# Attention with forget gates, then a GELU layer: another decay, another order of the first two batches

## The chip, the cores and the metric

The kernel runs on one core of a Trainium2 chip. The metric is the device time in microseconds, the median of several runs. In the text PE is TensorE (PEld its weight loads), DVE is VectorE, ACT is ScalarE, POOL is GpSimd, and SP is the engine that issues most of the plain DMAs.

## What is computed

Eight batches of causal attention with a decay, eight heads of 64 numbers, 576 positions; then two dense layers with an exact GELU between them on all 4608 rows. The reference, cut:

```python
scores = q @ k.T / sqrt(D)                       # q, k, v: (8, 8, 576, 64); f: (8, 8, 576)
cum    = cumsum(log(clip(f, 1e-4, 1.0)), -1)
decay  = cum[..., :, None] - cum[..., None, :]
attn   = softmax(where(causal, -1e9, scores + decay))
x      = (attn @ v) as rows of 512               # 8 heads side by side
h      = x @ w_in                                # (512, 2048)
out    = (0.5 * h * (1 + erf(h / sqrt(2)))) @ w_out   # (2048, 512)
```

In a softmax row the part of the decay that depends on the query cancels. So both kernels only weigh the key side: each row of v, and the column of ones beside it that yields the sum of the row, is multiplied by a weight of its key, and the division at the end takes out any common factor.

## The kernel before, as far as it is touched

Names. A pair `i` is two heads; `scores(b, i, t)` makes score tile `t` (of four) of pair `i`, keys on the partitions, in one of two score buffers in PSUM, and its exponential on ACT. Causal masks are either added by PE inside the tile (two small products with `key_of` and `after` for each 128-wide diagonal block) or cut out by POOL after the exponential (`affine_select`). `attend` is AV, 15 products of 65 columns for a head; `normalize` divides on DVE; `to_xT` transposes x for the dense layer. gemm1 is the first dense layer, gemm2 the second.

The decay:

```python
nc.vector.tensor_scalar(f_sb, f_sb, 1e-4, 1.0, Alu.max, Alu.min)
nc.scalar.activation(lf, f_sb, Act.Ln)
nc.vector.tensor_tensor_scan(cum, ones, lf, 0.0, Alu.mult, Alu.add)
# ... cut: in first_attention(), after the transposes of pair 0
nc.scalar.activation(wk, cum, Act.Exp, bias=cum[:, S // 2 : S // 2 + 1], scale=-1.0)
```

The second half of batch 0's attention:

```python
transposes_first(0, 3, 0, m_psum, "m")
scores(0, 2, 0)
transposes_first(0, 3, 1, m_psum, "m")     # PE transposes, then a DVE copy into kT[3]
weigh_v(0, 0, nc.vector)                   # one tensor_tensor of 640 columns
weigh_v(0, 1, nc.vector)
gate(0, 4)                                 # POOL reads v, so what follows waits for it
load_w_in(0); load_w_in(1)
weigh_v(0, 2); weigh_v(0, 3)               # POOL
load_w_in(2)
# ... cut
load_v(1, 0, 4)
load_w_in(3)
load_qk_tokens(1, 0, 4); load_qk_tokens(1, 4, 8)
load_w_out(0)
scores(0, 2, 1)
heads = [(i, h) for i in range(3) for h in range(2)]
for i, t in ((2, 2), (2, 3), (3, 0), (3, 1), (3, 2), (3, 3)):
    scores(0, i, t)
    attend_head(*heads.pop(0))
```

While gemm1 of batch 0 runs (its last quarter), POOL and SP do this:

```python
behind(qk_of[1][0], H - 1)                 # POOL reads the last head of q: waits for its landing
nc.gpsimd.memset(v_sb[:, 4:8, 0, 0:1], 0.0)
load_v(1, 4, 8)                            # SP, behind that memset
weigh_v(1, 0)
load_w_out(1)
weigh_v(1, 1)
load_qk_tokens(2)
```

Batch 1's attention, cut:

```python
tiles(0, 0)                                # score tiles 0 and 1 of pair 0
transposes(1, o_psum, "o"); transposes(2, m_psum, "m"); transposes(3, o_psum, "o")
tiles(0, 2)
take(fill, 2)                              # two products of gemm2_first(0)
tiles(1, 0); run(0); tiles(1, 2)           # run(i): AV of both heads of pair i
take(fill, 4)
weigh_v(1, 2)
tiles(2, 0); run(1)
weigh_v(1, 3)
tiles(2, 2)
take(fill, 4)
tiles(3, 0)
# ... cut: x of pairs 0 and 1 transposed, two more of gemm2
tiles(3, 2)
# ... cut
run(2)
take(fill, 4)
av(3, 0)
to_xT(b, 2, nc.scalar.copy, ps=both[:, 0, 0:XC])   # both: a score buffer
av(3, 1)
gemm1_begin(1, both)
```

`gemm2_first(0)` takes 16 products of 512 columns for batch 0 here: the first eight of sixteen blocks of w_out for two of four row tiles. The rest is done in batch 2's attention by `gemm2_second` (the other eight blocks for those two tiles, in halves of 64 rows) and `gemm2_rows(0, PLAN_0)` (all sixteen for the other two).

Of the kernel before, what the change touches and what calls it, by code (L numbers as in the profile page):

```python
# [15 lines left out]
P = 128  # L16
S = 576
# [36 lines left out]
def kernel(  # L54
# [100 lines left out]
    e4 = [consts.tile([P, 2, 448], BF16, name=f"e4{i}") for i in range(4)]  # L155
    for t in e4:
        nc.gpsimd.memset(t[:, :, 0:D], 0.0)
    diagonal(ident_fp, Alu.not_equal, 1.0, 0)
    load_qk_tokens(0, 6, 8)
# [20 lines left out]
    ones = consts.tile([BH, S], FP32)  # L180
    lf = f_sb
    cum = consts.tile([BH, S], FP32)
    wk = f_sb
    nc.vector.memset(ones, 1.0)
    nc.vector.memset(wT[0:D, 4, :], 0.0)
    nc.vector.tensor_scalar(f_sb, f_sb, 1e-4, 1.0, Alu.max, Alu.min)
    nc.scalar.activation(lf, f_sb, Act.Ln)
    nc.vector.memset(v_sb[0:D, :, 4, :], 0.0)
    nc.vector.tensor_tensor_scan(cum, ones, lf, 0.0, Alu.mult, Alu.add)
    spark = consts.tile([1, 1], FP32)  # L190
    nc.scalar.activation(spark, ones[0:1, 0:1], Act.Exp)

    def warm_up(n):

        ps = m_psum.tile([P, TC], FP32, tag="m", name="ps_w")
        for _ in range(n):
            nc.tensor.matmul(ps, warm[:, 0:P], warm, start=True, stop=True)
# [4 lines left out]
    def transposes_first(b, i, which, pool, tag):  # L202

        src = qk_of[b][which]
        ps = pool.tile([P, JT, PT], BF16, tag=tag, name="ps_f")
        for j in range(JT):
            for h in range(2):
                nc.tensor.transpose(
                    ps[h * D : (h + 1) * D, j, :],
                    src[:, 2 * i + h, j * D : (j + 1) * D],  # L210
                    ident_bf[:PT, :PT],
                )

        dst = (qT, kT)[which][i].rearrange("d (p j) -> d p j", j=JT)
        src = ps.rearrange("d j p -> d p j")
        if b or i:
            nc.vector.tensor_copy(dst, src)
        elif which:
            nc.vector.tensor_copy(dst[:, 0 : PT // 2], src[:, 0 : PT // 2])
            nc.scalar.copy(dst[:, PT // 2 :], src[:, PT // 2 :])  # L220
        else:
            nc.scalar.copy(dst, src)
# [41 lines left out]
    def weigh_v(b, i, eng=nc.gpsimd):  # L264

        hs = slice(2 * i, 2 * i + 2)
        bh = b * H + 2 * i
        w = wT[:, :, bh : bh + 2].rearrange("p n h -> p h n")
        eng.tensor_tensor(  # L269
            vw(b)[:, hs, :, 0:D],  # L270
            v_sb[:, hs, :, :],
            w.unsqueeze(3).to_broadcast([P, 2, NBLK, D]),
            Alu.mult,
        )
        if b:
            eng.tensor_copy(vw(b)[:, hs, :, D], w)
# [3 lines left out]
    def scores(b, i, t):  # L280
        on_pe = b == 0 or (b == 1 and i == 0)
# [42 lines left out]
    def attend(b, i, h, ms):  # L324
        if (b, i, h) not in o_of:
            o_of[b, i, h] = o_psum.tile([P, NBLK, D + 1], FP32, tag="o", name="o")
        o = o_of[b, i, h]
        for m in ms:
            for n in range(m + 1):
                t, c = where(n, m)  # L330
                nc.tensor.matmul(  # L331
                    o[:, m, :],
                    e_of[b, i, t][:, h, c : c + P],
                    vw_of[b][:, 2 * i + h, n, :],
                    start=(n == 0),
                    stop=(n == m),
                )
# [114 lines left out]
    PLAN_0 = [(2, "o", 16 * "r"), (3, "m", 14 * "r" + 2 * "n")]  # L452
# [57 lines left out]
    def gemm2_first(c):  # L510

        pss = [
            m_psum.tile([P, d_model], FP32, tag="m", name="ps2") for _ in range(2)
        ]
        for kq in (0, 4):
            for ts in range(2):
                for kt in range(kq, kq + 4):
                    nc.tensor.matmul(  # L518
                        pss[ts],
                        g_of[c][kt][:, ts * P : (ts + 1) * P],  # L520
                        w_out_sb[:, kt, :],
                        start=(kt == 0),
                        stop=(kt == 7),
                    )
                    if kt == 7:
                        ot_of.append(
                            o_pool.tile([P, d_model], FP32, tag="ot", name="ot")
                        )
                        copy = nc.scalar.copy if ts else nc.vector.tensor_copy
                        copy(ot_of[ts], pss[ts])  # L530
                    yield

    def gemm2_second(c):

        for ts, pool, tag in ((0, o_psum, "o"), (1, m_psum, "m")):
# [3 lines left out]
            for kt in range(8, n_ff):  # L539
                for r in range(2):  # L540
                    rows = slice(r * D, (r + 1) * D)
                    nc.tensor.matmul(  # L542
                        banks[r],
                        g_of[c][kt][rows, ts * P : (ts + 1) * P],
                        w_out_sb[rows, kt, :],
                        start=(kt == 8),
                        stop=(kt == n_ff - 1),
                    )
                if kt == n_ff - 1:
                    nc.vector.tensor_tensor(ot_of[ts], ot_of[ts], banks[1], Alu.add)  # L550
                    sum_out(c, ts, ot_of[ts], banks[0])
                yield

    def gemm2_third():
        yield from gemm2_second(0)
        yield from gemm2_rows(0, PLAN_0)
# [18 lines left out]
    def first_attention():  # L575
# [6 lines left out]
        def attend_head(i, h):  # L582
            attend(0, i, h, (0, 1, 2, 3, 4))
# [4 lines left out]
        nc.scalar.activation(  # L588
            wk, cum, Act.Exp, bias=cum[:, S // 2 : S // 2 + 1], scale=-1.0
        )  # L590
        warm_up(2)
        scores(0, 0, 0)
        scores(0, 0, 1)
        transposes(1, m_psum, "m")
        scores(0, 0, 2)
        psw = o_psum.tile([P, NBLK, BH], FP32, tag="o", name="psw")
        for n in range(NBLK):
            nc.tensor.transpose(
                psw[:, n, :], wk[:, K0[n] : K0[n] + P], ident_fp[:BH, :BH]
# [8 lines left out]
        transposes(2, m_psum, "m")  # L608
        scores(0, 1, 1)
        scores(0, 1, 2)  # L610
# [3 lines left out]
        transposes_first(0, 3, 1, m_psum, "m")  # L614
        weigh_v(0, 0, nc.vector)
# [8 lines left out]
        load_v(1, 0, 4)  # L624
# [5 lines left out]
        heads = [(i, h) for i in range(3) for h in range(2)]  # L630
        for i, t in ((2, 2), (2, 3), (3, 0), (3, 1), (3, 2), (3, 3)):
            scores(0, i, t)
            attend_head(*heads.pop(0))
# [87 lines left out]
    def second_attention():  # L721
# [23 lines left out]
        transposes(1, o_psum, "o")  # L745
        transposes(2, m_psum, "m")
        transposes(3, o_psum, "o")
        tiles(0, 2)
# [4 lines left out]
        take(fill, 4)  # L753
        weigh_v(1, 2)
# [11 lines left out]
        tiles(3, 2)  # L766
        behind(qk_of[2][1], H - 1)
# [4 lines left out]
        av(3, 0)  # L772
        both = s_psum.tile([P, 2, 1024], BF16, tag="s", name="ps_x2")
        to_xT(b, 2, nc.scalar.copy, ps=both[:, 0, 0:XC])
        av(3, 1)
# [4 lines left out]
    for b in range(B):  # L780
# [8 lines left out]
        for ffb in range(4 if b < 2 else 5, n_ff):  # L789
            gemm1(b, ffb, ps=spare() if b > 1 and ffb in (7, 8) else None)  # L790
            if b == 0:
# [3 lines left out]
                if ffb == 12:  # L795
                    behind(qk_of[1][0], H - 1)
                    nc.gpsimd.memset(v_sb[:, 4:8, 0, 0:1], 0.0)
                    load_v(1, 4, 8)
                    weigh_v(1, 0)
                    load_w_out(1)  # L800
                    weigh_v(1, 1)
                    load_qk_tokens(2)
# [43 lines left out]
```

## Time and profile before

| what | value |
|---|---|
| time, median of 3 | 337.49 us (337.18 to 338.54) |
| span of the profiled execution | 335.5 us |
| busy time of DVE, ACT, POOL in the span | 181.2, 209.2, 122.4 us |
| bytes moved by DMA | 44.16 MB, 132 GB/s on average |
| gemm1 of batch 0 starts | 22.97 us |
| gemm1 of batch 1 starts | 55.69 us |

How to read it. The page gives each engine's busy time and, in 40 equal slices of the span, its busy share in tenths. A matmul's record is longer than the time until the next one may start[...]; so a busy PE is not PE at its peak, and the distance between starts tells more. A table by stretch gives busy time between two moments, counted from the start of the span. The timeline lists instructions in order; in brackets stands how long the engine was idle before it, and which engine, line and tile ended that wait. Where several things were waited for, only the last is named. For a DMA the trace has the time of issue and the time of landing.

### The profile page before, as it was taken

To read this page: it belongs to the slowest core of one execution; us is meant where nothing else is said; L and a number is where in the kernel's file an instruction comes from. 1 tells how busy PE (TensorE), PEld (TensorE's weight loads), DVE (VectorE), ACT (ScalarE), POOL (GpSimd) and SP (SyncE) were. 2 spreads that over 40 slices of the span, in tenths; PEclk is the share of its full clock that TensorE was granted. 3 is DMA by queue.
4 is the path that set the end of the run, shared out by engine and by line. 5 is a ranking of instruction groups with operands and counts; after the bars stand their busy time and mean duration, and the time that the engine had idled before them with its cause. 6 is when DMAs were issued, how large, how long until landed. Compare 5 with 4: busy or idle time off the path is not lost.

```text
span 335.5 us, 7820 instructions
## 1 busy us (share of the span) xinstructions
PE 326.8 (97%) x3161; PEld 171.2 (51%) x3161; DVE 181.2 (54%) x414; ACT 209.2 (62%) x299; POOL 122.4 (36%) x250
## 2 busy tenths in 40 slices
PE   8799989999999999999999999999999999999995
PEld 3574546445554456445644565446544654444443
DVE  4770456684358945894589547964696550020011
ACT  6977797773734787378827891788378846404600
POOL 8190286038437044723463343624351420000000
PEclk9999999999999999999999999999999999999998
DMA  7999999989999799599949698689800241011013
GB/s 113 188 166 191 206 172 165 193 157 169 206 197 177 119 198 189 102 141 148 224 120 141 136 179 174 87 158 211 140 35 2 83 64 61 0 66 62 0 41 84
DMA packets 104627, 44.16 MB, mean 132 GB/s; under 512 B 83408, under 2 KB 100048, under 8 KB 104592
## 3 DMA queue, kind: packets, MB, share of 16 engines
q1 hardware_dynamic: 87296, 29.52, 46.4%
q0 software_dynamic: 16896, 13.63, 27.6%
q8 instruction: 24, 0.39, 0.5%
q10 hardware_dynamic: 400, 0.52, 0.4%
q14 instruction: 11, 0.09, 0.1%
HBM read 36.85 MB, written 9.44 MB: 138 GB/s over the span
## 4 chain that ended last, share of the span: by engine, by line
PE 83%; DMA 10%; POOL 3%; issue 1%; ACT 1%; DVE 1%; SPq 0%; POOLq 0%; DVEq 0%; ACTq 0%
PE ps L386 33%; PE ps L482 26%; PE ps L422 8%; PE o L331 7%; PE s L300 6%; DMA w_out_sb<-in_moe_w_out_dram 6%; DMA xT<-x 2%; DMA v_sb<-in_v_dram 2%; PE ps L542 1%; PE ps L518 1%; POOL q L108 1%; POOL k L108 1%; ACT e L310 1%; POOL vw L269 0%; SPq L120 0%
## 5 line engine op out<-in xcount | busy, mean ns | idle before, releaser
L406 ACT ACTIVATE g<-ps 128x512 bf16<-128x512 f32 x144 | 82.1, 601 | 83.7 <-PE ps L386 83.7
L310 ACT ACTIVATE e<-s 128x896 bf16<-128x896 f32 (+2 forms) x128 | 100.1, 835 | 20.9 <-PE s L300 18.2
L386 PE MATMUL ps<-xT,w_in_sb 128*128 128x512 bf16 x512 | 112.7, 379 | 0.1
L482 PE MATMUL ps<-w_out_sb,g 64*128 64x512 bf16 (+1 forms) x711 | 108.1, 377 | 0.0
L386 PEld LDWEIGHTS <-w_in_sb 128*128 128x128 bf16 x576 | 55.9, 98 | 67.8 <-issue 2.1
L312 POOL TENSOR_SCALAR_AFFINE_SELECT e<-e 128x256 bf16<-128x256 bf16 (+1 forms) x135 | 49.3, 386 | 86.9 <-ACT e L310 86.6
L482 PEld LDWEIGHTS <-g 64*128 64x128 bf16 (+1 forms) x711 | 39.4, 95 | 34.7 <-issue 4.2
L269 POOL TENSOR_TENSOR vw<-v_sb,wT 128x640 bf16<-128x640 f32 x30 | 38.7, 1290 | 26.0 <-DMA v_sb<-in_v_dram 14.7
L300 PE MATMUL s<-qT,kT 64*128 64x320 bf16 (+4 forms) x384 | 43.8, 276 | 2.2 <-ACT e L310 1.3
L250 DVE COPY kT<-tk 64x288 bf16<-64x288 bf16 x96 | 43.9, 458 | 2.3 <-DMA tk<-k 0.7
L250 DVE COPY qT<-tq 64x288 bf16<-64x288 bf16 x96 | 38.8, 404 | 3.7 <-DMA tq<-q 2.3
L490 DVE COPY ot<-ps 128x512 f32<-128x512 f32 x20 | 13.8, 692 | 47.2 <-PE ps L482 47.2
L331 PEld LDWEIGHTS <-e 128*128 128x128 bf16 x960 | 34.5, 98 | 8.6 <-POOL e L312 2.5
L331 PE MATMUL o<-vw,e 128*128 128x65 bf16 x960 | 37.4, 194 | 0.5 <-DVE vw L269 0.5
L345 DVE TENSOR_TENSOR x<-o,r 128x320 bf16<-128x320 f32 x64 | 31.5, 492 | 3.3 <-DMA xT<-x 1.1
L431 DVE COPY ot<-ps 128x512 f32<-128x512 f32 (+2 forms) x9 | 5.7, 633 | 49.6 <-PE ps L422 49.6
L300 PEld LDWEIGHTS <-kT 64*128 64x128 bf16 x384 | 19.6, 94 | 24.1 <-issue 7.6
L422 PE MATMUL ps<-w_out_sb,g 128*128 128x512 bf16 (+2 forms) x144 | 28.0, 355 | 0.0
L422 PEld LDWEIGHTS <-g 128*128 128x128 bf16 x144 | 13.5, 98 | 14.5
L344 DVE RECIPROCAL r<-o 128x5 f32<-128x5 f32 x64 | 12.1, 189 | 12.2 <-PE o L331 12.1
L502 DVE TENSOR_TENSOR ot<-ot,ps 128x512 f32<-128x512 f32 x22 | 15.1, 685 | 1.1
L386 PE MATMUL ps<-tails,w_in_sb 128*128 128x512 bf16 x64 | 14.3, 378 | 0.0
(69 smaller groups left out, 137.5 us busy)
## 6 DMA issues: line engine op xcount, KB each, us to landing
out_dram<-ot SPq DMA_DIRECT2D x32, 256.0 KB, 2.5
v_sb<-in_v_dram SPq DMA_DIRECT2D x24, 256.0 KB, 4.6
q<-in_q_dram POOLq DMA_DIRECT2D x6, 576.0 KB, 6.3
k<-in_k_dram POOLq DMA_DIRECT2D x6, 576.0 KB, 8.2
v_sb<-in_v_dram SPq DMA_DIRECT2D x22, 128.0 KB, 4.6
w_in_sb<-in_moe_w_in_dram POOLq DMA_DIRECT2D x4, 512.0 KB, 8.2
w_out_sb<-in_moe_w_out_dram POOLq DMA_DIRECT2D x4, 512.0 KB, 8.6
q<-in_q_dram POOLq DMA_DIRECT2D x4, 144.0 KB, 4.5
```

Source lines behind the costliest of these rows:

```text
L250: nc.vector.tensor_copy(rows[:, odd], src[odd * D : (odd + 1) * D, 2 * i + h].rearrange("d j p -> d p j"),)
L269: eng.tensor_tensor(vw(b)[:, hs, :, 0:D], v_sb[:, hs, :, :], w.unsqueeze(3).to_broadcast([P, 2, NBLK, D]), Alu.mult,)
L300: nc.tensor.matmul(to, *ab, start=half < 0, stop=half == 1 or not masked)
L310: nc.scalar.activation(et[:, :, z:c], st[:, :, z:c], Act.Exp, scale=scale)
L312: nc.gpsimd.affine_select(out=et[:, :, c0 + z : c0 + P], in_=et[:, :, c0 + z : c0 + P], compare_op=Alu.is_ge, fill=0.0, base=z, pattern=[[ ...
L331: nc.tensor.matmul(o[:, m, :], e_of[b, i, t][:, h, c : c + P], vw_of[b][:, 2 * i + h, n, :], start=(n == 0), stop=(n == m),)
L345: nc.vector.tensor_tensor(x_of[b, i][:, :, h, :], o[:, :, 0:D], r.unsqueeze(2).to_broadcast([P, NBLK, D]), Alu.mult,)
L386: nc.tensor.matmul(ps, w_in_sb[:, kt, ffb * P : (ffb + 1) * P], src[:, kt, 0:TC], start=(kt == 0), stop=(kt == n_dm - 1),)
L406: nc.scalar.activation(g_of[c][ffb], ps, Act.Gelu)
L422: nc.tensor.matmul(pss[ts][:, c0:c1], g_of[c][kt][:, ts * P : (ts + 1) * P], w_out_sb[:, kt, c0:c1], start=(kt == 0), stop=(kt == n_ff - 1),)
L482: nc.tensor.matmul(banks[r], g_of[c][kt][rows, ts * P : (ts + 1) * P], w_out_sb[rows, kt, :], start=kt == (steps.index("r") if r else 0), ...
L502: nc.vector.tensor_tensor(ot, ot, bank, Alu.add)
```

## The change

It has several parts, all in the first two batches and in the order of gemm2 of batch 0.

- The decay is a running product from the last position to the first, started at 2 to the 80th: one scan on DVE, with no logarithm and no exponential. It is meant to free ACT.
- Of pair 0's weighing the four whole blocks of v go first, then the last block; both go ahead of the copy of kT of pair 3. The AV of batch 0 is done two heads at a time, the first one after score tile (2, 2), those of pair 1 in the other PSUM pool.
- Memsets move from POOL to DVE, and loads change places: v of heads 2 and 3 of batch 1 later, w_out's second quarter after both weighings, k of batch 2 after q and in the middle of batch 1.
- `gemm2_first` uses only the first quarter of w_out, for all four row tiles; `gemm2_second` does the remaining twelve blocks of each. The number of products stays.
- In batch 1 score tiles 2 and 3 of pair 0 come before pair 3's transposes, the last pair is masked by PE, its AV is done in one go, and ACT loads the Gelu table right after the last exponential.

The diff, cut to its core (`...` marks cuts):

```diff
-    e4 = [consts.tile([P, 2, 448], BF16, name=f"e4{i}") for i in range(4)]
-    for t in e4:
-        nc.gpsimd.memset(t[:, :, 0:D], 0.0)
+    load_qk_tokens(0, 6, 8)
     diagonal(ident_fp, Alu.not_equal, 1.0, 0)
-    load_qk_tokens(0, 6, 8)
...
+    nc.scalar.activation(spark, none[0:1, 0:1], Act.Exp)
+    nc.vector.memset(decay[:, S - 1 : S], 2.0**80)
...
-    nc.scalar.activation(lf, f_sb, Act.Ln)
-    nc.vector.tensor_tensor_scan(cum, ones, lf, 0.0, Alu.mult, Alu.add)
...
-        on_pe = b == 0 or (b == 1 and i == 0)
+        on_pe = b == 0 or (b == 1 and i in (0, HP - 1))
...
         transposes(0, o_psum, "o")
-        nc.scalar.activation(
-            wk, cum, Act.Exp, bias=cum[:, S // 2 : S // 2 + 1], scale=-1.0
-        )
-        warm_up(2)
+        nc.vector.tensor_tensor_scan(
+            decay[:, S - 2 :: -1], f_sb[:, S - 1 : 0 : -1], none[:, 0 : S - 1],
+            2.0**80, Alu.mult, Alu.add,
+        )
+        warm_up(2, 2 * P)
...
-        transposes_first(0, 3, 1, m_psum, "m")
-        weigh_v(0, 0, nc.vector)
+        copy = transposes_first(0, 3, 1, m_psum, "m", late=True)
+        weigh_v(0, 0, nc.vector, 0, NBLK - 1)
+        weigh_v(0, 0, nc.vector, NBLK - 1)
+        copy()
         weigh_v(0, 1, nc.vector)
...
-        load_v(1, 0, 4)
+        load_v(1, 0, 2)
...
-        for i, t in ((2, 2), (2, 3), (3, 0), (3, 1), (3, 2), (3, 3)):
-            scores(0, i, t)
-            attend_head(*heads.pop(0))
+        scores(0, 2, 2)
+        for ms in ((0, 1, 2, 3), (4,)):
+            for h in range(2):
+                attend(0, 0, h, ms)
+        ... normalize, scores(0, 2, 3), scores(0, 3, 0)
+        for h in range(2):
+            attend_head(1, h, m_psum, "m")
+        scores(0, 3, 1)
+        scores(0, 3, 2)
+        for h in range(2):
+            attend_head(2, h)
+        scores(0, 3, 3)
...
         tiles(0, 0)
-        transposes(1, o_psum, "o")
-        transposes(2, m_psum, "m")
+        transposes(1, m_psum, "m")
+        transposes(2, o_psum, "o")
+        tiles(0, 2)
         transposes(3, o_psum, "o")
-        tiles(0, 2)
...
         take(fill, 4)
+        load_qk_tokens(2, which="k")
         weigh_v(1, 2)
...
         tiles(3, 2)
+        nc.scalar.activation(warm[0:1, 0:1], warm[0:1, 0:1], Act.Gelu)
...
-        av(3, 0)
+        run(3)
         both = s_psum.tile([P, 2, 1024], BF16, tag="s", name="ps_x2")
         to_xT(b, 2, nc.scalar.copy, ps=both[:, 0, 0:XC])
-        av(3, 1)
...
-                    nc.gpsimd.memset(v_sb[:, 4:8, 0, 0:1], 0.0)
+                    nc.gpsimd.memset(v_sb[:, 2:8, 0, 0:1], 0.0)
+                    load_v(1, 2, 4)
                     load_v(1, 4, 8)
                     weigh_v(1, 0)
+                    weigh_v(1, 1)
                     load_w_out(1)
-                    weigh_v(1, 1)
-                    load_qk_tokens(2)
+                    load_qk_tokens(2, which="q")
```

In `gemm2_first` the loop over two halves of eight blocks for two row tiles becomes a loop over two pairs of row tiles with four blocks each; in `gemm2_second` the loop over two row tiles with eight blocks becomes one over four row tiles with twelve, and `PLAN_0` goes.

## The prediction

> **What bounds the kernel now.** The page is read first, its busy shares and its slices, to see whether there is one bound or several.
>
> ```profile
> PE 326.8 (97%) x3161; PEld 171.2 (51%) x3161; DVE 181.2 (54%) x414; ACT 209.2 (62%) x299; POOL 122.4 (36%) x250
> ...
> PE   8799989999999999999999999999999999999995
> ```
>
> TensorE (PE) is at 9 or more in all slices but the first two, the sixth (42 to 50 us) and the last. So the table of busy time by stretch comes next; I chose the stretches at the ends of stages.
>
> ```profile
> core 0: us, PE busy (x) PEld busy (x) DVE busy (x) ACT busy (x) POOL busy (x), PEclk, DMA share, GB/s
> 0.00:5.20 5.20, 3.94 (x9) 1.19 (x9) 2.69 (x9) 2.42 (x3) 3.94 (x10) 1.00 0.55 85
> ...
> 7.90:16.00 8.10, 6.21 (x143) 4.58 (x144) 5.96 (x11) 8.02 (x12) 1.31 (x3) 1.00 1.07 204
> 16.00:23.00 7.00, 6.99 (x172) 6.07 (x172) 5.66 (x16) 5.52 (x8) 6.93 (x11) 1.00 1.02 155
> 23.00:38.10 15.10, 15.10 (x98) 6.82 (x94) 2.41 (x6) 10.30 (x17) 1.81 (x4) 1.00 1.22 185
> 38.10:44.00 5.90, 4.87 (x117) 3.25 (x117) 4.41 (x7) 5.37 (x8) 4.51 (x8) 1.00 1.14 204
> 44.00:55.70 11.70, 11.06 (x178) 7.02 (x177) 5.85 (x17) 9.81 (x14) 10.35 (x24) 1.00 1.15 176
> 55.70:70.10 14.40, 14.40 (x74) 6.36 (x71) 10.31 (x32) 10.32 (x17) 0.81 (x2) 1.00 1.23 187
> ```
>
> The reader is to see two things. From 55.7 us on (and in 23 to 38) PE is busy the whole stretch, and the change takes no product away there: whatever is won before 55.7 us passes to the end one to one, and nothing else is to be had. And before that PE's idle time is 1.26 + 1.89 + 0.01 + 1.03 + 0.64 = 4.8 us, of which the first 1.26 us (waiting for the first q) is not touched. In 7.9 to 16 us ScalarE (ACT) is the bound, 8.02 of 8.10 us; in 44 to 55.7 ACT, GpSimd (POOL) and PE are all near full.
>
> The timeline tells what ends those idle times. Columns: start, length, engine, line, operation; in brackets the idle time before and what ended it.
>
> ```profile
> 7.20 0.77 ACT L588 ACTIVATE f_sb<-cum 64x576 f32<-64x576 f32 x1
> 7.88 8.63 ACT L310 ACTIVATE e<-s 128x896 bf16<-128x896 f32 x11
> 14.46 0.76 DVE L217 COPY kT<-ps_f 128x576 bf16<-128x576 bf16 x1 [0.19 <-PE ps_f L208]
> 15.13 1.55 DVE L269 TENSOR_TENSOR vw<-v_sb,wT 128x640 bf16<-128x640 f32 x2
> 16.01 0.63 PE L331 MATMUL o<-vw,e 128*128 128x65 bf16 x15 [0.51 <-DVE vw L269]
> 42.71 0.61 PE L518 MATMUL ps<-w_out_sb,g 128*128 128x512 bf16 x2 [0.44 <-DMA w_out_sb<-in_moe_w_out_dram]
> 47.60 1.28 POOL L269 TENSOR_TENSOR vw<-v_sb,wT 128x640 bf16<-128x640 f32 x1 [0.22 <-POOL e L312]
> 51.33 1.73 POOL L312 TENSOR_SCALAR_AFFINE_SELECT e<-e 128x256 bf16<-128x256 bf16 x5
> ```
>
> The first exponential starts at the end of the decay's own exponential; eleven run without a gap; the first AV waits 0.51 us for the weighing on VectorE (DVE), which itself stood behind the kT copy; the first gemm2 product of batch 1 waits 0.44 us for w_out; and POOL has a train of weighings and selects up to 53.1 us.
>
> [...] the fourth of v(1) needed 15.1 us from issue to landing, against 4.5 us for a v block at 6.0 us. [...] Where 64-row scores follow a 512-column product the starts lie 0.31 us apart, against 13.81/64 = 0.216 us within a run of gemm1; so about 0.1 us a switch.
>
> **The change part by part.**
>
> 1. *Decay by products.* Ln, one table load and the exponential L588 go; the scan (1.35 us) stays on DVE, now behind the kT copy that ends at 6.88, so it ends near 8.25, in time for the decay's transposes (9.11 before). On ACT the qT copy can start when its transposes end, near 6.0 instead of 6.15, and the kT half after it; scores (0,0) end some 0.15 us sooner, and their exponential no longer stands behind L588 (0.13 us: scores end at 7.71, exponential at 7.88, and elsewhere it follows in 0.04). Sum: the chain of eleven exponentials starts **0.3 us** sooner.
>
> 2. *Pair 0 weighed in two parts, AV grouped.* The four whole v blocks have landed at 13.77, the fifth at 14.75. The first part [...] starts when the qT copy of pair 3 ends, about 14.0, ends 14.7; the second [...] waits for 14.75 and ends 15.05. kT of pair 3 follows, to 15.8. PE reaches the first AV when score tile (2,2) is out, 15.43 before and 15.15 with part 1; the weight is there, so AV starts at 15.2 instead of 16.01. AV in pairs of heads also saves three switches there and back. Following PE and ACT in turn (AV of a pair 0.95 us, scores 0.3 to 0.47, two score buffers, each exponential 0.7 to 0.9) I get gemm1 of batch 0 at 22.0 instead of 22.97: **0.9 to 1.0 us**, part 1 included. w_in is no new wait: its quarters landed at 21.58, 24.09, 27.82 and 32.10 and are used from 22.0, 26, 29.5 and 33.
>
> 3. *DMA order.* Half of v(1, heads 0 to 3), 1152 packets, leaves the stretch before 38 us. The landing of q and k heads 4 to 7 (38.34 and 40.13) and of w_out's first quarter (42.66) should come about 2 us sooner, estimated from the v blocks' pace there: blocks of 512 packets landed 2.8 us apart beside the weights. Then gemm2 finds its quarter (needed near 41.8, there near 41), and the 0.44 us wait goes. Only one quarter is needed for all sixteen products, so the second quarter is out of the way.
>
> 4. *Batch 1.* Score tiles 2 and 3 of pair 0 ahead of pair 3's transposes take away ACT's 0.21 us gap at 42.03. The masks of the last pair cost PE nine pairs of 64-column products: scores of pair 3 in batch 0 took 0.47 + 0.30 us for tiles 0 and 1, unmasked ones in batch 1 0.63 together, so five of the pairs cost 0.14; for all nine I take **0.25 us** on the path. What they take from POOL, five selects of 0.35 us, was done at 54.28, before AV (3,0) at 54.46, so at the old pace it delayed nothing. The early Gelu table and the two more DVE copies lie beside other work. gemm2's later 48 steps keep their number and their time.
>
> Sum of what PE could win: 1.0 + 0.2 + 0.3 (w_out, partly the same idle time as the 0.2) - 0.25, about **1.1 us**.
>
> 5. *What takes part of it back: POOL.* weigh_v(1,1) now needs v heads 2 and 3, issued only when q's second half has landed (near 36.3), sharing with k and w_out; I put their landing at 42.1. [...] From there: weighing with its cast 1.42, issue of w_out and q 1.6, five selects 1.8, issue of k 0.8 (new at this place), weighing 1.42, three selects 1.0, weighing 1.42, two selects 0.7: 10.1 us, so the last select that AV (2) needs is done at 52.2, against 52.02 before. AV (2) stood at 52.64; a PE that is 1.0 us sooner comes at 51.7 and waits 0.5 us. So of 1.1 us I keep **0.6 to 0.7**.
>
> **The rivals.** *(a) POOL's chain becomes the bound outright*: if v lands at 43 or later, the selects end after 53.1 and batch 1 gives all of the early gain back, even 0.3 us more; 337.5 to 337.8. For it: POOL is busy 10.35 of 11.70 us there. *(b) The chain has slack*: v lands by 41, since blocks of half the size run as soon as w_out is through (before, after w_out landed, v blocks came 0.45 us apart); then the whole 1.1 us stays, 336.4. *(c) The early gain is hidden anyway*, since batch 1 starts on DMA: k of heads 4 to 7 landed at 40.13 and transposes waited 0.2 us for it. That speaks for a wait only if part 3 brings nothing: 337.2. *(d) The front wins more*, since fewer switches count for more than 0.1 us each: 336.0.
>
> **Range and chances.** 337.49 - 0.65 = 336.84. (b) and (a) bound it at 336.2 and 337.8; the three times before lay 1.4 us apart, so I widen to 335.7 and 338.0. Two per cent are 6.75 us, more than all of PE's idle time before 55.7 us, and the losses that I see are under 1 us: within 2% is all but certain.
>
> **What would show it.** The first exponential near 7.6; the first AV near 15.2 with no wait for vw; gemm1 of batch 0 near 22.0; gemm2 of batch 1 with no wait for w_out; weigh_v(1,1) on POOL starting near 42, with its wait put down to v's DMA; AV (2) waiting for a select of POOL; gemm1 of batch 1 near 55.0 (55.69 before), and from there every stage shifted by the same amount. Wrong would be: gemm1 of batch 0 later than 22.5 (the front mis-timed), weigh_v(1,1) far from 42 (the DMA order mis-timed), or a shift that changes after 70 us (a stage that I took as untouched).

## The result, and the profile after

The changed kernel takes **340.42 us** (median of six runs, 338.86 to 340.93), the kernel before beside it 337.62 (337.18 to 338.54). The ratio is 1.0075, interval 1.0052 to 1.0099: slower by 2.8 us, where 0.65 us of gain had been predicted. A ratio leaves out executions more than 1.5% above the fastest of the same kernel, a median takes them all. Where is it lost? The start of gemm1 in each batch says it (us; first gemm1 product of the batch; the tails are the last 64 rows of every batch, taken together at the end):

| | batch 0 | 1 | 2 | 3 | 4 | 5 | tails |
|---|---|---|---|---|---|---|---|
| before | 22.97 | 55.69 | 101.56 | 136.38 | 171.20 | 206.02 | 303.59 |
| after | 22.36 | 55.54 | 102.67 | 139.12 | 173.94 | 209.41 | 306.69 |
| after minus before | -0.61 | -0.15 | +1.11 | +2.74 | +2.74 | +3.39 | +3.10 |

Up to batch 1 the changed kernel is ahead. The loss arises between 55.5 and 209 us, in stages in which the diff changes only the order of gemm2's products for batch 0. The page's busy shares do not show it; these are its lines for PE:

```profile
PE 327.6 (97%) x3179; PEld 172.3 (51%) x3179; DVE 183.2 (54%) x422; ACT 206.7 (61%) x297; POOL 120.0 (35%) x241
PE   8899899999998999999999999999999999999995
```

The share is 97% as before, and one slice behind batch 1, the thirteenth (102 to 110 us), fell to 8. So the table by stretch comes next, for stretches that the prediction showed.

```profile
core 0: us, PE busy (x) PEld busy (x) DVE busy (x) ACT busy (x) POOL busy (x), PEclk, DMA share, GB/s
...
38.10:44.00 5.90, 4.83 (x137) 3.65 (x132) 4.26 (x7) 5.27 (x8) 2.17 (x4) 1.00 0.78 162
44.00:55.70 11.70, 11.04 (x177) 6.99 (x174) 7.29 (x20) 10.37 (x15) 8.57 (x18) 1.00 1.18 172
```

Look at the column DMA share, second from the right. Before, it stood at 1.02 to 1.23 in six of the seven stretches shown; above 1 the recorded times of the packets add up to more than the stretch, so they overlap on the engines. After, in 38 to 44 us, it is 0.78 (1.14 before), and POOL is busy 2.17 us there instead of 4.51. A finer cut gives 0.90 against 1.18 for 44 to 50 us. (1.14 - 0.78) x 6 + (1.18 - 0.90) x 6 = 3.8 us of packet time for each engine that these two stretches held in the kernel before and do not hold here; in the first of them the rate fell from 204 to 162 GB/s. In 50 to 56 us the share is higher, 1.45 against 1.10. POOL's timeline tells why; the kernel before first.

```profile
41.07 0.81 POOL L176 DMA_DIRECT2D w_out_sb<-in_moe_w_out_dram  x1
...
43.27 0.84 POOL L108 DMA_DIRECT2D q<-in_q_dram  x1
44.09 0.78 POOL L108 DMA_DIRECT2D k<-in_k_dram  x1
...
77.23 1.73 POOL L312 TENSOR_SCALAR_AFFINE_SELECT e<-e 128x256 bf16<-128x256 bf16 x5
```

The same instructions in the changed kernel:

```profile
42.69 1.28 POOL L270 TENSOR_TENSOR vw<-v_sb,wT 128x640 bf16<-128x640 f32 x1 [3.73 <-DMA v_sb<-in_v_dram]
...
44.05 0.82 POOL L173 DMA_DIRECT2D w_out_sb<-in_moe_w_out_dram  x1
44.85 0.80 POOL L108 DMA_DIRECT2D q<-in_q_dram  x1
45.65 1.73 POOL L313 TENSOR_SCALAR_AFFINE_SELECT e<-e 128x256 bf16<-128x256 bf16 x5
47.32 0.77 POOL L108 DMA_DIRECT2D k<-in_k_dram  x1
...
81.10 1.72 POOL L313 TENSOR_SCALAR_AFFINE_SELECT e<-e 128x256 bf16<-128x256 bf16 x5
```

POOL stands 3.73 us before the second weighing of batch 1, until v of heads 2 and 3 has landed. The loads of w_out's second quarter, q and k of batch 2 stand behind that weighing in POOL's program and are issued with it: w_out at 44.05 instead of 41.07. From there the delay goes from queue to queue (us, landing):

| | before | after |
|---|---|---|
| w_out, second quarter | 47.20 | 49.97 |
| q, k of batch 2 | 51.31, 54.23 | 52.92, 56.89 |
| last DMA transpose of k (batch 2), in SP's queue | 67.30 | 70.22 |
| last block of v (batch 2), in SP's queue behind it | 72.71 | 76.42 |
| q, k of batch 3, in POOL's queue behind two weighings of that v | 82.08, 85.71 | 86.77, 92.04 |
| last transpose of x (batch 2), in SP's queue | 101.93 | 106.34 |

PE meets it in four places. The first AV of batch 2 in the kernel before, with the score product behind it:

```profile
81.62 1.11 PE L331 MATMUL o<-vw,e 128*128 128x65 bf16 x30
82.66 0.36 PE L300 MATMUL s<-qT,kT 64*128 64x448 bf16 x2
```

And all four places in the changed kernel, from three stretches of its timeline:

```profile
81.72 0.23 PE L332 MATMUL o<-vw,e 128*128 128x65 bf16 x2
82.53 1.32 PE L332 MATMUL o<-vw,e 128*128 128x65 bf16 x28 [0.58 <-POOL e L313]
83.78 0.36 PE L301 MATMUL s<-qT,kT 64*128 64x448 bf16 x2
...
103.54 0.81 PE L387 MATMUL ps<-xT,w_in_sb 128*128 128x512 bf16 x3 [0.49 <-DMA xT<-x]
105.17 1.02 PE L387 MATMUL ps<-xT,w_in_sb 128*128 128x512 bf16 x4 [0.82 <-DMA xT<-x]
...
175.46 0.81 PE L387 MATMUL ps<-xT,w_in_sb 128*128 128x512 bf16 x3 [0.49 <-DMA xT<-x]
```

The bracket gives the idle time by modelled ends (in the kernel before the record of a 512-column product of gemm1 is 0.38 us long, while 64 of them in a row take 13.81 us, 0.216 us each); the distance of starts says what it costs. The first AV of batch 2 took from 81.72 to the next score at 83.78, 2.06 us, against 1.04 before: 1.0 us. The three gemm1 products, two in batch 2's gemm1 and one in batch 4's, started 0.87, 1.20 and 0.87 us after the one before them instead of 0.22: 0.65 + 0.98 + 0.65. Together 3.3 us of the 3.54 that lie between -0.15 and the +3.39 of batch 5; the other 0.26 us arose in batch 2 as well, nearly all ahead of its first AV (26.18 us from gemm1 of batch 1 to there, 25.93 before). From gemm1 of batch 5 to that of batch 6 the kernel before takes 0.3 us longer than the changed one (35.12 against 34.84), which makes the last figure 3.10. That these four waits are nearly all of the loss is read from the trace; that the order of the loads is their cause needs runs.

### The profile page after: what moved, and what is told of

It reads as the page before. It is cut to its first block, busy times and chain, and to the rows that moved or that the text cites. A ratio compares the mean times of both kernels' runs of the same rounds, so it can differ in the third digit from the quotient of the medians.

```text
span 338.8 us, 7859 instructions
## 1 busy us (share of the span) xinstructions
PE 327.6 (97%) x3179; PEld 172.3 (51%) x3179; DVE 183.2 (54%) x422; ACT 206.7 (61%) x297; POOL 120.0 (35%) x241
## 4 chain that ended last, share of the span: by engine, by line
PE 82%; DMA 6%; SPq 4%; ACT 2%; POOL 2%; issue 1%; DVE 1%; POOLq 0%; ACTq 0%
PE ps L387 32%; PE ps L482 24%; PE ps L423 8%; PE o L332 8%; PE s L301 7%; SPq L237 3%; DMA k<-in_k_dram 3%; ACT e L311 2%; DMA xT<-x 2%; DMA v_sb<-in_v_dram 2%; PE ps_w L194 1%; PE ps_f L207 1%; SPq L120 1%; POOL e L313 1%; POOL vw L270 1%
## 5 line engine op out<-in xcount | busy, mean ns | idle before, releaser
L482 PE MATMUL ps<-w_out_sb,g 64*128 64x512 bf16 (+1 forms) x649 | 100.4, 377 | 0.0
L313 POOL TENSOR_SCALAR_AFFINE_SELECT e<-e 128x256 bf16<-128x256 bf16 (+1 forms) x130 | 47.1, 384 | 82.8 <-ACT e L311 82.7
L482 PEld LDWEIGHTS <-g 64*128 64x128 bf16 (+1 forms) x649 | 36.4, 95 | 31.3 <-issue 3.8
L490 DVE COPY ot<-ps 128x512 f32<-128x512 f32 x18 | 12.4, 691 | 45.2 <-PE ps L482 45.2
```

The source lines that it names most:

```text
L313: nc.gpsimd.affine_select(out=et[:, :, c0 + z : c0 + P], in_=et[:, :, c0 + z : c0 + P], compare_op=Alu.is_ge, fill=0.0, base=z, pattern=[[ ...
L482: nc.tensor.matmul(banks[r], g_of[c][kt][rows, ts * P : (ts + 1) * P], w_out_sb[rows, kt, :], start=kt == (steps.index("r") if r else 0), ...
```

## The experiments

The theory: POOL's wait for v (3.73 us) holds up a train of loads, DMA time stays idle (a share of 0.78 and 0.90), and the queues, in which the loads of the table landed in the order of their issue, carry the delay into batches 2 to 4. Ratios are to the kernel before, with 95% intervals.

### Which part of the change costs: compute or order

**Batch 0's part alone**, put into the kernel before (decay as a product, pair 0 weighed in two parts, AV in pairs; batch 1, all loads and gemm2 as before):

```diff
-        load_v(1, 0, 2)
+        load_v(1, 0, 4)
-                    load_v(1, 2, 4)
-                    weigh_v(1, 1)
                     load_w_out(1)
+                    weigh_v(1, 1)
-                    load_qk_tokens(2, which="q")
+                    load_qk_tokens(2)
... # from after; and batch 1's masks, order and gemm2_first of before
```

> The kernel before with the batch 0 part of the change alone: product decay, memsets on VectorE, the two-part weighing, the copy behind it, AV by pairs. The DMA order, gemm2 and batch 1 are those of before. gemm1 of batch 0 should start near 22.4 as in the changed kernel (22.97 before). If what is won there passes on, as the prediction said, gemm1 of batch 1 starts 0.5 us sooner and the time is 337.0 to 337.3. If batch 1 starts on DMA (k of heads 4 to 7 and w_out's first quarter), the 0.6 us are waited away there: 337.5 to 337.8.

Measured: 337.42 us, 0.9974 (0.9942 to 1.0006). The interval just holds 1, so it was measured again:

> The kernel before with batch 0's part of the change alone (decay as a product, pair 0 weighed in two parts, AV in pairs), measured once more, now in five rounds, since the first ratio, 0.9974 with an interval from 0.9942 to 1.0006, leaves open whether it gains. Theory (the kernel before is set by its DMA landings after the front, so a faster front is eaten up by waits for k and w_out): ratio 0.999 to 1.001. Rival (the front's gain passes to the end at least in part): ratio 0.9965 to 0.9985.

Measured: 337.61 us, **0.9992 (0.9969 to 1.0016)**. If the front gains at the end, it gains at most about 0.3%; the first run's suggestion was not borne out. In the trace of the first of the two runs gemm1 of batch 0 started at 22.28 (22.97 before), and then PE stood 0.92 us between starts for batch 1's k and 1.07 us for w_out's first quarter, here by its record:

```profile
42.66 0.60 PE L519 MATMUL ps<-w_out_sb,g 128*128 128x512 bf16 x2 [0.85 <-DMA w_out_sb<-in_moe_w_out_dram]
```

The product of w_out starts at 42.66, where it started at 42.71 in the kernel before. The front was not what that point waited for. Of the 0.69 us, 0.36 were left at gemm1 of batch 1 (55.33), and in batch 2 PE stood 0.71 us between starts for a sum on DVE.

In the trace of the second run gemm1 of batch 0 started at 23.05, no sooner than before. So the front's gain is not steady even at its own end: in the traces of eleven of the thirteen runs with this front that start lies between 22.11 and 23.43, with a median of 22.54. In the two latest PE stood 1.18 and 1.04 us for w_in's first quarter, which landed at 23.39 and 23.31 (21.58 before).

**The rest alone**: the changed kernel with batch 0's compute as before.

```diff
-        nc.vector.tensor_tensor_scan(decay[:, S - 2 :: -1], f_sb[:, S - 1 : 0 : -1], ...)
+        nc.scalar.activation(wk, cum, Act.Exp, bias=cum[:, S // 2 : S // 2 + 1], scale=-1.0)
... # weighing and AV order of batch 0 as in before
```

> The changed kernel with the batch 0 part of before (decay by logarithm and exponential, weighing in one part, AV head by head); DMA order, gemm2 and batch 1 as changed. The complement of the kernel with the front alone. If the loss is made by the new order of loads and issues (T1), it is all here: gemm1 of batch 0 at 23.0, k of batch 2 lands at 56.5 to 57.5, gemm1 of batch 2 and of batch 3 about 3 us later than before, time 340.2 to 341.2. A rival, that the faster front itself makes the collision (loads meet work that comes too soon), expects 338.5 or less.

Measured: 339.67 us, 1.0064 (1.0037 to 1.009): below the 340.2 to 341.2 expected, but not the rival's 338.5 or less. w_out's second quarter was issued at 43.91, the DMA share was 0.80 and 0.91 in 38 to 44 and 44 to 50, and PE waited for xT in batches 2 and 4. Most of the loss is there without the front.

**All the compute, the old order of loads**: the changed kernel in which only the loads go back.

```diff
-        load_v(1, 0, 2)
+        load_v(1, 0, 4)
-                    load_v(1, 2, 4)
-                    weigh_v(1, 1)
                     load_w_out(1)
-                    load_qk_tokens(2, which="q")
+                    weigh_v(1, 1)
+                    load_qk_tokens(2)
-        load_qk_tokens(2, which="k")
```

> The kernel after with the whole order of loads of the kernel before: v(1) of heads 0 to 3 early, w_out's second quarter between the two weighings, q and k of batch 2 together behind them; everything that changes on PE, ACT and DVE in both batches stays. If the whole loss lies in the order of loads: k of batch 2 lands near 54 to 54.5 us, batches 2 and 3 take 45.8 and 34.8 us from gemm1 to gemm1, time 337.0 to 338.0, the same as before. If w_out's first quarter, then later again (near 42.7), now holds up all of batch 1's gemm2 or the score tiles: gemm1 of batch 1 starts 0.3 to 0.7 us later than before and the time is 338.0 to 338.5. If the compute part itself costs: over 338.5.

Measured: 338.08 us, **1.0002 (0.9974 to 1.003)**. Within that interval, some 0.3% or 1 us, the whole loss goes. The table by stretch of this run has the DMA share of the kernel before again, 1.17 in 38 to 44 us, and 1.20 in the next six, and POOL's second weighing starts 0.84 us after the w_out load, with no wait:

```profile
38.00:44.00 6.00, 4.47 (x108) 3.02 (x105) 4.08 (x7) 4.99 (x7) 3.57 (x6) 1.00 1.17 211
44.00:50.00 6.00, 5.55 (x91) 3.45 (x90) 3.75 (x10) 5.03 (x7) 5.13 (x12) 1.00 1.20 190
...
41.99 0.81 POOL L173 DMA_DIRECT2D w_out_sb<-in_moe_w_out_dram  x1
42.83 1.29 POOL L270 TENSOR_TENSOR vw<-v_sb,wT 128x640 bf16<-128x640 f32 x1
```

From gemm1 to gemm1 batches 2 and 3 take 45.81 and 34.83 us (before 45.87 and 34.82; after 47.13 and 36.45). The front's lead was waited away here too: PE stood 0.92 us for batch 1's k and 0.28 us for w_out, gemm1 of batch 1 started at 56.58, 0.89 us later than before, and k of batch 2 landed at 55.31, a microsecond later than I expected. That is the second of the outcomes expected, w_out's first quarter late again, and 338.08 us lies on its border. So the compute part shows neither a cost nor a gain at the end that is clear of the interval.

**Only POOL's masks back**: the last pair of batch 1 masked by POOL again.

```diff
-        on_pe = b == 0 or (b == 1 and i in (0, HP - 1))
+        on_pe = b == 0 or (b == 1 and i == 0)
```

> The changed kernel with the last pair of batch 1 masked by POOL as before. The prediction gave the TensorE masks a cost of 0.25 us on the path and no gain. Then gemm1 of batch 1 starts 0.1 to 0.3 us sooner than in the changed kernel (55.5), unless POOL, which ends its earlier selects at 52.6, now holds up AV of pair 3; in that case it starts 0.2 to 0.6 us later. The time stays at 340 to 341 in both cases, since the later chain hangs on DMA.

Measured: 339.41 us, 1.0015 (0.9986 to 1.0044). For the whole kernel this is inconclusive: the times lay between 336.58 and 341.68, and the profiled execution is the longest of them. In it batch 1, from gemm1 of batch 0 to its own, took 33.20 us at full clock, against 33.18 in the changed kernel. As far as one trace tells, PE's masks cost about nothing there.

### Is it a lack of DMA time?

**Less to load**: three quarters of w_out are not loaded at all, and gemm2 reads the first quarter in their place, so the output is another; all products stay. Once with the changed kernel, once with the kernel before:

```diff
-        load_w_out(2)
-        load_w_out(3)
... # load_w_out(1) too; and in gemm2:
-                        w_out_sb[rows, kt, :],
+                        w_out_sb[rows, kt % 4, :],
```

> The changed kernel with the second, third and fourth quarters of w_out not loaded; gemm2 reads the first quarter in their place, so products, copies and stores keep their number and size, and only the second factor is another (3 x 512 KB less on the DMA engines). Theory: up to 75 us the DMA engines are the bound, and the change leaves them idle from 38 to 50 us (share 0.78 and 0.90 against 1.14 and 1.18 before), which is where its loss comes from. Without the three quarters k of batch 2 lands near 52.5 to 53.5 and v of batch 2 before 71, so the waits in batches 2 and 3 go, and the time is 336.8 to 337.4. Rival: the waits there come from the order of TensorE's and VectorE's own work (gemm2 in groups of twelve); then 339.5 or more also here.

> The kernel before with the same three quarters of w_out not loaded and the first read in their place. If DMA is no bound on it, since TensorE hides it, as the prediction read its profile, then it gains little: 336.9 to 337.6. Set against the changed kernel with the same quarters left out it shows what the change is worth where DMA has room: I expect the changed kernel to be 0.1 to 0.5 us faster there. If before gains 1 us or more, DMA is on its path too.

Measured: the changed kernel 337.78 us, 1.0008 (0.9982 to 1.0034); the kernel before 338.15 us, 1.0009 (0.999 to 1.0028). Without that megabyte and a half the changed kernel has no wait in batches 2 and 3 (45.82 and 34.82 us; last transposes landed at 61.83, v at 67.86) and is level with before; the kernel before gains nothing. The two times lie 0.4 and 0.55 us above the ranges expected, and k of batch 2 landed at 54.50, a microsecond late, but the rival's 339.5 us is far off. So the loads of the kernel before arrive early enough, and the changed kernel's do not. This is the theory's strongest support beside the old order: the same products, less in the queues, no loss. It also narrows the theory: the DMA share is 0.77 in 38 to 44 us here as well, since POOL's wait is still there. So idle DMA time alone cost nothing here; what counts is how much is loaded behind it.

### One load at a time

**k of batch 2 right behind q** again:

```diff
-                    load_qk_tokens(2, which="q")
+                    load_qk_tokens(2)
-        load_qk_tokens(2, which="k")
```

> The changed kernel with k of batch 2 loaded right behind q, as before, instead of in the middle of batch 1's attention. Theory T1 (the queue's start): w_out's second quarter, q and k of batch 2 run one behind the other in POOL's DMA queue; in the changed kernel that train starts at 44.05 us (41.07 before) since POOL stands in weigh_v(1,1), which waits for v of heads 2 and 3; k lands when the train has run, whatever its own issue time. T1 expects k to be issued 1.6 us sooner, yet to land at 56.0 to 56.9 (56.89 in the changed kernel) and a time of 339.7 to 340.6. Theory T2 (the place of k's issue): k lands by as much sooner as it is issued, near 55.2, and the time falls to 338.7 or less.

Measured: 340.08 us, 1.0049 (1.003 to 1.0067). k was issued 1.7 us sooner (45.61) and landed no sooner, 57.23 against 56.89: it stood in the queue instead of on POOL, as T1 expected. The rival that made k's place the cause falls.

**w_out's second quarter last**, with quarters 3 and 4, behind k:

```diff
-                    load_w_out(1)
+        load_w_out(1)
         load_w_out(2)
```

> The changed kernel with w_out's second quarter loaded behind k of batch 2, with the third and fourth; it is needed only in batch 2's attention. k keeps its late place. T1 expects the train to lose its first car: q near 49.5, k near 53.5, the DMA transposes of q and k and then v of batch 2 about 3 us sooner, AV of pair 0 in batch 2 without a wait for POOL's selects, and a time of 337.0 to 338.0. T2 (k's place alone) expects k to land at most 1 us sooner, and 339.5 or more. T3 (the loss is made in batch 2 by the new order of gemm2 and its stores) expects 340 or more whatever k does.

Measured: 339.01 us, 1.0037 (1.0017 to 1.0058). With 512 KB less ahead of them q landed at 50.06 and k at 53.67, sooner than in the kernel before, and the AV of batch 2 no longer waited. Yet gaps of 0.90 and 0.59 us for xT stayed, at 102 and 172 us: v of batch 2, now behind three quarters of w_out, landed at 75.08 (76.42 after, 72.71 before). About half of the loss is given back; T1's 337.0 to 338.0 was not reached.

**v of batch 2 ahead of its transposes** in SP's queue:

```diff
+        load_v(2)
         transpose_dma(2, 0, 4)
         transpose_dma(2, 4, 8)
-        load_v(2)
```

> The changed kernel with v of batch 2 loaded ahead of the DMA transposes of q and k in SP's queue, instead of behind them. k stays late (56.9 or later). T1 says that k's delay reaches TensorE through SP's order: transposes, then v, then weighing, the next q and k issue and the selects on POOL. Taken out there, AV of pair 0 in batch 2 does not wait, and the later waits of gemm1 in batch 2 for the DMA transposes of x go too: 337.0 to 338.2. A rival, that late transposes of q and k themselves hold up the scores of batch 2, expects 340 or more.

Measured: 351.29 us, 1.0271 (1.0201 to 1.0341). In the profiled execution, of 354.42 us, v landed by 67.2 instead of 76.4, but the last transpose of k was issued at 70.98 and landed at 84.56, and PE stood 3.80 us for the copy of kT behind them and 8.86 us for a sum on DVE. My expectation failed; the rival, which named just this, held. Turned round in this way, SP's order costs some 9 us by that ratio.

**Only w_out's load back ahead of the second weighing:**

```diff
                     weigh_v(1, 0)
-                    weigh_v(1, 1)
                     load_w_out(1)
+                    weigh_v(1, 1)
```

> The kernel after with one line moved: the load of w_out's second quarter stands between weigh_v(1,0) and weigh_v(1,1) again, as in the kernel before; k of batch 2 stays in the middle of batch 1. Theory (DMA engines idle because the train of loads begins behind POOL's wait for v): w_out's second quarter is issued near 39.5 us instead of 44.05 and lands near 45.5 to 47 (49.97 after), the DMA share in 38 to 50 us is back at 1.0 to 1.1, q of batch 2 lands near 50.5 to 51.5, k near 54.5 to 55.5, gemm1 of batch 2 waits 0.5 us or less for xT; v of heads 2 and 3 of batch 1 shares its stretch with w_out and lands up to 1 us later (43 to 43.5), which costs up to 0.5 us in batch 1; time 338.3 to 339.3. Rival (only the place of k behind q counts): k still lands near 56.9 and the time stays at 340.0 or more.

Measured: 340.43 us, 1.007 (1.0045 to 1.0095). I expected 338.3 to 339.3, and that fell. The load was issued at 39.05 and landed at 45.41, as expected, and batches 2 and 3 took 45.82 and 34.82 us, with no loss at all. But v of heads 2 and 3, now beside it, landed at 45.73 (42.52 after), and POOL shows the price:

```profile
39.05 0.81 POOL L173 DMA_DIRECT2D w_out_sb<-in_moe_w_out_dram  x1
45.90 1.27 POOL L270 TENSOR_TENSOR vw<-v_sb,wT 128x640 bf16<-128x640 f32 x1 [6.04 <-DMA v_sb<-in_v_dram]
```

A wait of 6.04 us, selects from 48.11, and AV of batch 1 waited for them, 1.36 and 0.91 us between starts. The loss moved from batch 2 into batch 1. k of batch 2 landed at 56.25 here, hardly sooner than in the changed kernel, and nothing waited behind it, since gemm1 of batch 1 started 2.5 us later too (58.02 against 55.54).

### Other orders

Three orders, each with w_out's second quarter last: v of heads 0 to 3 early again, with q and k of batch 2 together; q and k ahead of the second weighing; and the same with POOL first made to wait for v of head 3 (`gate`).

```diff
-        load_v(1, 0, 2)                  # first
+        load_v(1, 0, 4)
-                    weigh_v(1, 1)        # second; third: gate(3, 4) ahead of the load
+                    load_qk_tokens(2)
+                    weigh_v(1, 1)
```

> The changed kernel with v of heads 0 to 3 of batch 1 early as before, q and k of batch 2 issued together in before's place, and w_out's second quarter behind them. weigh_v(1,1) then does not wait for a late v, and the train of q and k starts at once and has no w_out ahead. T1 expects q and k to land at 47 to 52, the transposes and v of batch 2 earlier than before, no wait in batches 2 and 3, and gemm2's first product to wait for w_out's first quarter as in the kernel with the front alone (1.07 us there). Time 336.4 to 337.2, better than before. If the waits in batches 2 and 3 stem from w_out's quarter being loaded among the transposes and v (T4), 338 or more.

> The changed kernel, v of heads 2 and 3 late as it has it, but q and k of batch 2 issued ahead of weigh_v(1,1), that is ahead of the wait for that v, and w_out's second quarter behind them. T1 expects k to land at 48 to 52 and the later chain to be gone. The cost: v of heads 2 and 3 shares with q and k, weigh_v(1,1) starts at 44 or later instead of 42.7 and AV of pair 1 in batch 1 waits for POOL's selects, up to 1.5 us more than in the changed kernel. Sum: 337.0 to 338.5. T4 (w_out among the transposes) expects 338.5 or more.

> The changed kernel with q and k of batch 2 issued as soon as v of heads 2 and 3 has landed (POOL reads one of its elements first), ahead of weigh_v(1,1), and w_out's second quarter loaded with the third and fourth. v keeps its right of way, and the train of q and k starts 1.2 us sooner than where w_out's quarter alone was moved (43.90 there). Theory: q issued near 42.7, k lands near 52.4 (53.67 there, 54.23 before), AV of pair 1 in batch 1 as in the changed kernel, no wait of AV in batch 2, at most one short wait of gemm1 for x. Time 336.8 to 338.0.

Measured: 338.96 us, 1.0023 (1.0003 to 1.0044); 341.56, 1.0106 (1.0062 to 1.015); 339.29, 1.0033 (1.001 to 1.0055). All three are slower than expected. In all three batch 2 takes 45.82 us, as in the kernel before, and in all three batch 1 is longer: 35.21, 37.06 and 34.51 us from gemm1 to gemm1, against 32.72 before. In the first, w_out's first quarter landed at 44.33, PE waited 1.70 us for it, and its granted clock fell to 0.50 (see the last section). In the twelve of its twenty executions with a mean clock of 0.9975 or more the median is 337.83 us, against 337.79 for such executions of the kernel before; so what this order loses, it loses in executions in which the clock falls. In the second v stood behind q and k:

```profile
40.11 0.78 POOL L108 DMA_DIRECT2D k<-in_k_dram  x1
45.96 1.28 POOL L270 TENSOR_TENSOR vw<-v_sb,wT 128x640 bf16<-128x640 f32 x1 [5.07 <-DMA v_sb<-in_v_dram]
```

In the third AV of batch 1 waited 0.63 and 0.92 us for POOL's selects, and gemm1 of batch 2 0.99 us for x. No version tried beats the kernel before beyond its interval.

**What is settled**: the order of the loads makes the loss, to within 0.3% (1.0002 without it, 1.0064 with it and without the front). Of the places tried for the train none is good beside the late half of v: behind the weighing it comes too late for batch 2, ahead of it it makes v late for batch 1. **What stays open**: how much each load of the order takes by itself, since their effects do not add; and whether any of the front's 0.4 us or so (22.54 against 22.97) reaches the end, which these intervals cannot tell.

## Why the prediction was wrong, by its own steps

- **Step 1, decay: 0.3 us predicted, none came in this trace.** The first exponential starts at 7.94 (predicted 7.6; before 7.88). ACT's qT copy began at 5.95, near the 6.0 predicted, but k landed at 5.84 (5.75 before), its transposes began at 5.88, and the halves of kT were copied at 6.62 and 7.11, later than before (6.42 and 6.91). The path ran over k's landing and kT, not over L588. The mis-sized term is the 0.15 us for scores that end sooner: the last score product of the tile started at 7.80, 0.2 us later than before (7.60), and so the 0.13 us behind L588, which did go, could not show. One trace does not settle the size: in the eleven traces with the new front the first exponential starts between 7.49 and 8.05, with a median of 7.75.
- **Step 2, AV in pairs: right in kind, smaller.** These lines of the changed kernel's timeline answer to the ones shown of before:

```profile
7.94 8.71 ACT L311 ACTIVATE e<-s 128x896 bf16<-128x896 f32 x11 [0.44 <-PE s L301]
...
14.54 0.90 DVE L270 TENSOR_TENSOR vw<-v_sb,wT 128x512 bf16<-128x512 f32 x2
...
15.58 1.13 PE L332 MATMUL o<-vw,e 128*128 128x65 bf16 x30
```

  The first AV starts at 15.58 with no wait for vw (predicted 15.2; before 16.01). The two parts of the weighing, of 512 and 128 columns, took 0.69 and 0.29 us by their records and 0.90 us together, and the second ended at 15.44 (15.05 predicted, its author's estimate); one of 640 columns took 0.82. gemm1 of batch 0 starts at 22.36: 0.61 us of the 0.9 to 1.0; what is missing was missing when the first AV started (15.58 instead of 15.2). "w_in is no new wait" held here, but not in the two runs named above.
- **Step 3, w_out: right on the landing, wrong on the gain.** It landed at 41.13 (predicted near 41) and nothing waited for it. But of the 0.5 us that steps 3 and 4 promised (0.3 for w_out, 0.2 for ACT's gap) nearly none was won: PE was 0.61 us ahead of the kernel before at batch 1's first score product (37.87 against 38.48) and 0.65 at its first AV (43.22 against 43.87). The score tiles that were moved ahead of pair 3's transposes waited for exponentials, 0.83 and 0.24 us by the record.
- **Step 4, masks by PE: a cost of 0.25 us was allowed**; the run without them shows about none.
- **Step 5, POOL's chain in batch 1: right in its times, but it bit one pair sooner.** v of heads 2 and 3 landed at 42.52, and the weighing began at 42.69 with its wait put down to v's DMA (42.1 predicted); the last select that AV (2) needs ended at 52.60 (52.2). But AV (2) started at 52.40 with no wait in the record, where a wait of 0.5 us was predicted. The lead of 0.65 us had gone before, at AV (1); the kernel before first, then the changed one:

```profile
47.23 1.17 PE L331 MATMUL o<-vw,e 128*128 128x65 bf16 x30
48.34 0.36 PE L300 MATMUL s<-qT,kT 64*128 64x448 bf16 x2
...
46.58 0.24 PE L332 MATMUL o<-vw,e 128*128 128x65 bf16 x2
47.08 1.32 PE L332 MATMUL o<-vw,e 128*128 128x65 bf16 x28 [0.26 <-POOL e L313]
48.33 0.50 PE L301 MATMUL s<-qT,kT 64*128 64x448 bf16 x4
```

  In both kernels the last of pair 1's selects ended at 47.38 (46.97 + 0.41 and 45.65 + 1.73), and the next score product started at 48.33 or 48.34. The prediction's own times showed it: 42.1 + 1.42 + 1.6 + 1.8 = 46.9 for these selects, and an AV (1) that is 1.0 us sooner comes at 46.2. It followed the chain to AV (2) alone. gemm1 of batch 1 stands at 55.54 (55.0 predicted).
- **The step that failed** is the one ahead of all these: from 55.7 us on PE is busy the whole stretch, so "whatever is won before 55.7 us passes to the end one to one, and nothing else is to be had". It did not pass, and much was to be lost: behind 55.7 us the changed kernel lost 3.3 us in four waits. Busy PE in the kernel before shows only that its loads arrive in time, not by how much. The margin could have been read: the last of pair 0's selects in batch 2 ended at 77.23 + 1.73 = 78.96, and the AV that needs them started at 81.62, 2.7 us of slack. After, the selects end at 82.82, 3.9 us later. 3.9 - 2.7 = 1.2 us; the AV lost 1.0. Step 5 followed POOL's arithmetic to the end of batch 1 and left out what the same delay does to the three loads behind it. Rival (a) had POOL's delay too, but let it end in batch 1. Among its signs of being wrong the prediction named "a shift that changes after 70 us (a stage that I took as untouched)"; this is the one that came. (A slip beside it: the lower bound of 336.2 that is put down to (b) is not (b)'s own 336.4.)
- **The sign was in the table shown.** The DMA share stood above 1 in nearly every stretch up to 70 us, so there was little room to make a delay good. In this case it was passed on nearly whole: w_out's second quarter was issued 2.98 us and landed 2.77 us later, and the last blocks of v of batch 2 landed 3.71 us later.

On POOL a load waited for a weighing that waited for another load: w_out was issued at 44.05, once the weighing that had stood 3.73 us for v was done.

## What to carry to other kernels

Before moving a load, list what stands behind it in the same engine's program, DMA issues above all, and read the slack of each consumer from the trace; a busy bound engine says nothing of that slack. Where the DMA share stays above 1, as here (1.02 to 1.23 in six of the seven stretches shown of before), look at the queues as a second bound: here DMA time that was left idle (a share of 0.78 instead of 1.14) was paid for later, with 3.3 us of waits in stretches where the kernel before had PE busy throughout, as long as there was as much to load behind it. And before a load is split so that half comes later, look at what stands behind its consumer: here that was a train of three loads.

## What the hardware showed beyond that

In one run a wait of PE was followed by a second cost. In the first of the three other orders PE stood 1.70 us for w_out (1.49 us idle by the record), and of 38 to 44 us it was busy 3.70; then its granted clock fell. From the tables by stretch of that run:

```profile
46.00:47.00 1.00, 1.00 (x23) 1.00 (x21) 0.26 (x2) 1.00 (x2) 0.50 (x2) 0.50 1.25 192
```

The clock column (third from the right) is 0.99 from 44 to 45 us, 0.50 from 45 to 48, 0.81 from 48 to 49, and 1.00 again after that: 3 x 0.50 + 0.19 = 1.7 us of PE's work at full clock. That the wait caused it was not shown. It did not follow each such wait: in the run with w_out's load between the weighings PE was busy 3.89 us of 44 to 50 in the profiled execution and the clock stayed at 1.00. There the times of the other executions show it, though not where it fell: 14 of 22 had a mean clock under 0.9975, and the median of the other eight was 339.18 us, against 340.43 for all; of 181 runs of the kernel before 37 were below.
